# Turning of gathered rows in a mixture-of-experts kernel: the next tile's transposes ahead of a tile's last low parts, and one first output bank for every chunk

## The chip, the cores and the metric

The kernel runs on one core of one Trainium2 chip. The metric is the device time of one execution in microseconds (us), as the median over several executions; lower is better.

## The reference

The program is one attention layer with a sliding window, whose output feeds a mixture of experts with two experts per row. All arrays are float32.

```python
B, H, S, D = 8, 8, 576, 64                     # attention; window 64, causal
attn = softmax(where(mask, q @ k.T / sqrt(D), -1e9))
x = (attn @ v) as 4608 rows of 512
noisy = x @ w_gate + log1p(exp(x @ w_noise)) * noise     # 8 experts
top2 = two best experts of each row, with softmax weights top2_w
for e in range(8):
    for k in range(2):
        mask = top2[:, k] == e
        h = maximum(x[mask] @ w1[e], 0.0)                # 512 -> 1024
        out[mask] += top2_w[mask, k, None] * (h @ w2[e]) # 1024 -> 512
```

## The kernel before

**Attention and routing.** The first third of the program computes attention block by block, stores the rows `X` to DRAM and builds, per expert, the list of its rows. Neither part is touched by the change.

**Experts in chunks.** Each expert's rows are worked off in chunks: expert 0 in three (384, 384 and 448 rows), experts 1 to 7 in two each, 576 rows (chunk 0) and 640 rows (chunk 1). The loop at line 1116 runs over the chunks. Each chunk has two phases on TensorE: `up` (line 822, hidden layer, matmuls over half a chunk: 288 or 320 columns) and `down` (line 958, output layer, matmuls over 512 columns, one tile of 128 rows after the other; chunk 0's last tile has 64 rows). Every product is made of three matmuls on split operands: high times high, low times high, high times low. A "high part" is a copy of a float32 tile rounded to the fast matmul type, written by ScalarE; the "low part" is the difference, written by VectorE. The first layer of experts 1 to 7 uses a seven-product scheme for 2x2 blocks: `XH` and `XL` hold seven blocks (sums and differences of quarters of the rows, and the quarters themselves), and `PRODUCT` says which block meets which weight block.

**Gather and turn.** While `up` of a chunk runs, `gather` (line 670) fetches the next chunk's rows by an indirect DMA into `xg`, writes them to DRAM (`xs`) and reads them back in another layout (`xc`). While `down` of a chunk runs, `turn` (line 719) makes the next chunk's `XH` and `XL` from `xc`, tile by tile (five tiles; `q` is the tile, `m` its rows). Its two steps per tile are
- `f` (line 728): two 32x32-block transposes on VectorE, `xc` to `tq` (line 737);
- `g` (line 745): the first high part on ScalarE (749), a difference on VectorE (750), the first low part (751), two more differences (752, 753), then the second high part on ScalarE (755) and the second low part on VectorE (756). Blocks 0 to 2 come out of the first parts, blocks 3 to 6 out of the second.

`tq` has one buffer, taken anew for each tile; `up` takes the same buffer for its own sums.

**Order of the work.** The order on every engine is the order in which the program issues. `spread` (line 77) sets side work between the steps of a main loop: it lays the items of a list evenly over a stretch of the steps. `turn` returns a list of steps, and the loop at line 1116 lays it over `down`, from `free` to 0.86 of its steps, together with (in chunk 1) the last two quarters of the next expert's weight split: high parts at line 242, low parts at line 234, sums at line 264. Each engine works off its own instructions in that order.

**Banks.** PSUM has eight banks of 128x512: three `z` banks, `v`, `y`, two `d` banks and one for attention. `up` uses `v` and `y` for products of their own: the first product of a chunk (product 2) goes to `v`, the second (product 5) to `y`. The output tiles of `down` go round a ring of three: `d0`, `d1` and `y` (line 1108, `ring` at line 818). Their results are taken out by ScalarE (line 997; the 64-row tile by 999 on ScalarE and 1000, 1001 on VectorE) and added to DRAM by an indirect DMA of POOL (line 919). `turns["d"]` counts on from chunk to chunk, so that the first bank of a chunk differs.

```python
def ring(name):
    turns[name] += 1
    return BANKS[name][turns[name] % len(BANKS[name])]
```

Of the kernel before, what the change touches and what calls it, by code (L numbers as in the profile page):

```python
# [8 lines left out]
F32 = mybir.dt.float32  # L9
# [21 lines left out]
HALF = WIDE // 2  # L31
# [24 lines left out]
def chunks(e):  # L56
    return CHUNKS if e else FIRST


def tiles(e, c):  # L60
    n = chunks(e)[c]
    return [(q, min(128, n - q * 128)) for q in range(-(-n // 128))]
# [25 lines left out]
def tile_kernel(ctx, tc, qT, kT, vx, vT, wgx, noise, w1, w2, out):  # L88
# [611 lines left out]
    def turn_first(c):  # L700
        if not X0:
            X0.extend(exa.tile([128, 7, 2, HALF], F32R, name=x).rearrange("p a k n -> p (a k n)") for x in ("xh", "xl"))
        o = c % 2 * KD * FIRST[-1]
        xh, xl = (x[:, o:o + KD * FIRST[-1]].rearrange("p (k n) -> p k n", k=KD) for x in X0)
        XH[0, c], XL[0, c] = xh, xl
        cur = {}

        def f(q, m):
            y = cur[q] = turn_bank()[:, :KD * m].rearrange("p (k m) -> p k m", k=KD)
            for k in range(KD):  # L710
                nc.tensor.transpose(y[:, k], XG[0, c, q][:m, k * 128:k * 128 + 128], ident[:m, :m])

        def g(q, m):
            h, l = (x[:, :, q * 128:q * 128 + m] for x in (xh, xl))
            nc.scalar.activation(h, cur[q], AF.Copy)
            nc.vector.tensor_tensor(l, cur[q], h.bitcast(F32), op=OP.subtract)
        return [lambda q=q, m=m, x=x: x(q, m) for q, m in tiles(0, c) for x in (f, g)]

    def turn(e, c):
        if e == 0:  # L720
            return turn_first(c)
        todo = {}

        def begin():
            todo["h"] = XH[e, c] = exa.tile([128, 7, 2, HALF], F32R, name="xh")
            todo["l"] = XL[e, c] = exa.tile([128, 7, 2, HALF], F32R, name="xl")

        def f(q, m):
            if q == 0:
                begin()  # L730
            w = m // 2
            t = todo[q] = EXB["p"].tile([128, 4 * HALF], F32, name="tq", bufs=1)
            v = t[:, :16 * w].rearrange("p (s x) -> p s x", s=8)
            for h in range(2):
                d = v[:, 2 - 2 * h:4 - 2 * h].rearrange("p s (k x) -> p (s k) x", k=2).rearrange("p k (t c) -> p t k c", c=32)
                a = h * (CHUNKS[c] // 64) + 2 * q
                nc.vector.transpose(d, XC[e, c][:, a:a + w // 32].rearrange("p t (k c) -> p t k c", c=32))  # L737

        def parts(q, m, s0, s1):
            w = m // 2  # L740
            a = todo[q][:, s0 * 2 * w:s1 * 2 * w].rearrange("p (a x) -> p a x", x=w)
            return (a, *(x.rearrange("p a k x -> p (a k) x")[:, 2 * s0 - 2:2 * s1 - 2, q * 64:q * 64 + w]
                         for x in (todo["h"], todo["l"])))

        def g(q, m):
            w = m // 2
            v = todo[q][:, :16 * w].rearrange("p (s x) -> p s x", s=8)
            a, h, l = parts(q, m, 1, 4)
            nc.scalar.activation(h, a, AF.Copy)  # L749
            nc.vector.tensor_tensor(v[:, 4:6], v[:, 0:1].to_broadcast([128, 2, 2 * w]), v[:, 1:3], op=OP.subtract)  # L750
            nc.vector.tensor_tensor(l, a, h.bitcast(F32), op=OP.subtract)  # L751
            nc.vector.tensor_tensor(v[:, 6], v[:, 1], v[:, 5], op=OP.subtract)
            nc.vector.tensor_tensor(v[:, 7], v[:, 3], v[:, 6], op=OP.subtract)  # L753
            a2, h2, l2 = parts(q, m, 4, 8)
            nc.scalar.activation(h2, a2, AF.Copy)  # L755
            nc.vector.tensor_tensor(l2, a2, h2.bitcast(F32), op=OP.subtract)  # L756
        return [lambda q=q, m=m, x=x: x(q, m) for q, m in tiles(e, c) for x in (f, g)]

    pair = []

# [13 lines left out]
    EXB, BANKS = {}, {}  # L774
# [41 lines left out]
    late, turns = [], {"z": 0, "d": 0}  # L816
# [4 lines that stand above are left out]
# [106 lines left out]
    def down_first(c):  # L927
        e = 0
        hh, hl, ht = HH.pop((e, c))
        wt = GW[e, c]  # L930
        w2h, w2l = W2["h"], W2["l"]
        for q, m in tiles(e, c):
            y = exa.tile([128, XW], F32, name="xg", bufs=XB)[:, :DM]
            p = ring("d")
            if m == 128:
                sl = slice(q * 128, q * 128 + m)
                for f in range(KF):
                    nc.tensor.matmul(p, lhsT=hh[f][:, sl], rhs=w2h[:, f, :], start=(f == 0), stop=False)
                    nc.tensor.matmul(p, lhsT=hh[f][:, sl], rhs=w2l[:, f, :], start=False, stop=False)
                    nc.tensor.matmul(p, lhsT=hl[f][:, sl], rhs=w2h[:, f, :], start=False, stop=(f == KF - 1))  # L940
                    if f < KF - 1:
                        yield
                nc.scalar.activation(y, p, AF.Copy, scale=wt[:, q:q + 1])
            else:

                for f in range(KF):
                    t = ht[f].rearrange("p s t -> p (s t)")
                    nc.tensor.matmul(p, lhsT=t, rhs=w2h[:, f, :], start=(f == 0), stop=False)
                    nc.tensor.matmul(p, lhsT=t, rhs=w2l[:, f, :], start=False, stop=(f == KF - 1))
                    if f < KF - 1:  # L950
                        yield
                nc.scalar.activation(y[:m], p[m:2 * m], AF.Copy)
                nc.vector.tensor_tensor(y[:m], y[:m], p[:m], op=OP.add)
                nc.vector.tensor_scalar(y[:m], y[:m], wt[:m, q:q + 1], None, op0=OP.mult)
            add_rows(e, c, q, m, y)
            yield

    def down(e, c):
        if e == 0:
            yield from down_first(c)  # L960
            return
        wt = GW[e, c]
        hb = HH.pop((e, c))
        w2h, w2l = W2["h"], W2["l"]
        order = (0, 4, 1, 5, 2, 6, 3, 7)
        size = dict(tiles(e, c))
        steps = [(0, 0, 4), None, (0, 4, 6), (1, 0, 2), None, (1, 2, 6), (0, 6, 8), (1, 6, 8)]
        steps += [(q, 0, 8) for q in size if q > 1]
        P_ = {}
        for s in steps:  # L970
            if not s:
                yield from late.pop(0)
                continue
            q, i0, i1 = s
            m = size[q]
            if i0 == 0:
                P_[q] = ring("d")
            p = P_[q]
            for i in range(i0, i1):
                f = order[i]  # L980
                a, b = dict(start=(i == 0), stop=False), dict(start=False, stop=(i == KF - 1))
                if m == 128:
                    h, l = (hb[:, x, f, q * 128:q * 128 + 128] for x in range(2))
                    nc.tensor.matmul(p, lhsT=h, rhs=w2h[:, f, :], **a)  # L984
                    nc.tensor.matmul(p, lhsT=h, rhs=w2l[:, f, :], start=False, stop=False)  # L985
                    nc.tensor.matmul(p, lhsT=l, rhs=w2h[:, f, :], **b)  # L986
                else:
                    t = hb[:, 0, f, q * 128:q * 128 + 2 * m]
                    nc.tensor.matmul(p, lhsT=t, rhs=w2h[:, f, :], **a)
                    nc.tensor.matmul(p, lhsT=t, rhs=w2l[:, f, :], **b)  # L990
                if i < KF - 1:
                    yield
            if i1 < KF:
                continue
            y = exa.tile([128, XW], F32, name="xg", bufs=XB)[:, :DM]
            if m == 128:
                nc.scalar.activation(y, p, AF.Copy, scale=wt[:, q:q + 1])  # L997
            else:
                nc.scalar.activation(y[:m], p[m:2 * m], AF.Copy)
                nc.vector.tensor_tensor(y[:m], y[:m], p[:m], op=OP.add)  # L1000
                nc.vector.tensor_scalar(y[:m], y[:m], wt[:m, q:q + 1], None, op0=OP.mult)
            add_rows(e, c, q, m, y)
            yield
# [46 lines left out]
    for j in range(NT + 3):  # L1050
        if j == TURN:
            for q, f in enumerate(turn(0, 0)):
                aux.setdefault(j + q // 2, []).append(f)
# [53 lines left out]
    d, z, v, y = ([mps.tile([128, 512], F32, name=f"ps_{x}{q}") for q in range(k)] for x, k in zip("dzvy", (2, 3, 1, 1)))  # L1107
# [8 lines left out]
    for n, (e, c) in enumerate(work):  # L1116
        nxt = work[n + 1] if n + 1 < len(work) else None
        last = c == len(chunks(e)) - 1
# [171 lines left out]
```

## Time and profile before

| what | us |
|---|---|
| median of 3 runs | 1079.51 |
| the three runs | 1073.28, 1079.51, 1079.69 |
| profiled execution: span from its first to its last instruction | 1070.0 |
| TensorE busy in the span | 994.8 (93%) |
| VectorE busy | 715.2 (67%) |
| ScalarE busy | 521.8 (49%) |

The profile is of one execution. The list of runs does not name it apart: what is on record of its own time is its span, 3.3 us under the shortest run and 9.5 us under the median. Attention fills the span up to about 300 us; `up` of expert 1 starts at 332 us; the last matmul starts at 1058.6 us.

In the rows, PE is TensorE, DVE is VectorE, ACT is ScalarE, SP is the engine that issues plain DMAs. `L737` is line 737 of the kernel before. `ps_y<-xh,WH` is a matmul that writes bank `y` from `xh` and weights `WH`. A matmul's busy time overlaps the next one's: the distance between two starts is what a matmul costs in a stream.

### The profile page before, as it was taken

Reading aid. Unit: us, or ns where it says so; the run is one execution under the profiler, and the core shown is the slowest. Engines: PE = TensorE matmul, PEld = TensorE weight load, DVE = VectorE, ACT = ScalarE, POOL = GpSimd, SP = SyncE. Lnnn points to the kernel's source line nnn. Section 1 sums busy time; section 2 is a strip of 40 time slices with the busy share of each in tenths; the row PEclk is TensorE's granted clock in tenths of the full one; section 3 lists DMA queues with packets and bytes.
Section 4 is the critical chain, followed back from the end, with each engine's and each line's share of the span. In section 5 each row is a group of like instructions: output and inputs, shape, how many; then the busy total and the mean of one; then the engine's idle time right before and its main releaser. Section 6 shows DMA issues by size and latency. Waiting matters only on the chain.

```text
span 1070.0 us, 22034 instructions
## 1 busy us (share of the span) xinstructions
PE 994.8 (93%) x8433; PEld 882.8 (83%) x8433; DVE 715.2 (67%) x1804; ACT 521.8 (49%) x1305; POOL 338.5 (32%) x465
## 2 busy tenths in 40 slices
PE   8787878779999999999999999999999999999995
PEld 8676767668788898889898889898889897989894
DVE  5688888684276667666776677677666866686630
ACT  4885666432244444544463446354644554454430
POOL 5436636333223141413132213222322323132202
PEclk9998998989999999999999999999999999999998
DMA  9987887874357653665377626762765385537303
GB/s 340 364 259 230 252 257 239 273 230 113 49 131 193 168 115 65 188 169 119 61 204 162 149 25 206 162 145 30 230 136 140 43 244 124 125 69 209 45 2 51
DMA packets 107235, 168.94 MB, mean 158 GB/s; under 512 B 13360, under 2 KB 57648, under 8 KB 105328
## 3 DMA queue, kind: packets, MB, share of 16 engines
q1 hardware_dynamic: 89968, 126.96, 38.7%
q0 software_dynamic: 17152, 40.48, 20.8%
q8 instruction: 68, 1.11, 0.4%
q14 instruction: 47, 0.39, 0.1%
HBM read 110.08 MB, written 57.32 MB: 156 GB/s over the span
## 4 chain that ended last, share of the span: by engine, by line
PE 42%; DVE 30%; ACT 8%; DMA 8%; issue 8%; POOL 1%; SPq 1%; DVEq 0%; POOLq 0%; ACTq 0%
PE ps_z L841 4%; PE ps_z L843 4%; PE ps_z L842 4%; DVE tq L737 4%; DVE WL L234 3%; ACT xh L755 3%; DVE xl L756 3%; DMA xc<-xs 3%; DVE xl L751 2%; PE ps_d L985 2%; PE ps_d L984 2%; PE ps_d L986 2%; DVE ws L264 2%; DVE pt L358 2%; DMA xs<-xg 2%
## 5 line engine op out<-in xcount | busy, mean ns | idle before, releaser
L919 POOL DMA_INDIRECT out_dram<-xg,los x70 | 111.1, 1587 | 423.7 <-ACT xg L997 364.5
L853 ACT ACTIVATE hb<-tq 128x288 fp32r<-128x288 f32 (+1 forms) x168 | 77.1, 459 | 144.4 <-DVE tq L872 138.7
L841 PE MATMUL ps_z<-xh,WH 128*128 128x288 f32 (+1 forms) x448 | 137.4, 307 | 0.9
L842 PE MATMUL ps_z<-xl,WH 128*128 128x288 f32 (+1 forms) x448 | 135.6, 303 | 0.0
L843 PE MATMUL ps_z<-xh,WL 128*128 128x288 f32 (+1 forms) x448 | 135.6, 303 | 0.0
L872 DVE TENSOR_TENSOR tq<-ps_z,tq 128x288 f32<-128x288 f32 (+1 forms) x168 | 79.3, 472 | 81.8 <-PE ps_z L843 76.4
L985 PE MATMUL ps_d<-w2l,hb 128*128 128x512 f32 x328 | 127.9, 390 | 0.0
L984 PE MATMUL ps_d<-w2h,hb 128*128 128x512 f32 x328 | 127.8, 390 | 0.0
L986 PE MATMUL ps_d<-w2h,hb 128*128 128x512 f32 x328 | 127.7, 389 | 0.0
L857 DVE SCALAR_TENSOR_TENSOR hb<-tq,hb 128x320 fp32r<-128x320 f32 (+2 forms) x168 | 75.5, 449 | 37.6 <-ACT hb L853 34.2
L675 POOL DMA_INDIRECT xg<-xrows,lxs x70 | 71.1, 1016 | 83.7 <-DMA xs<-xg 39.0
L841 PEld LDWEIGHTS ps_z<-xh,WH 128*128 128x128 f32 x448 | 84.8, 189 | 5.2 <-DVE tq L872 3.8
L842 PEld LDWEIGHTS ps_z<-xl,WH 128*128 128x128 f32 x448 | 84.8, 189 | 1.1
L755 ACT ACTIVATE xh<-tq 128x512 fp32r<-128x512 f32 (+1 forms) x70 | 42.7, 611 | 87.9 <-DVE tq L753 87.9
L843 PEld LDWEIGHTS ps_z<-xh,WL 128*128 128x128 f32 x448 | 84.7, 189 | 0.0
L756 DVE TENSOR_TENSOR xl<-tq,xh 128x512 fp32r<-128x512 f32 (+1 forms) x70 | 46.6, 666 | 47.4 <-ACT xh L755 47.4
L395 ACT ACTIVATE x<-ps_o,r 128x80 f32<-128x80 f32 x288 | 67.0, 348 | 15.2 <-DVE r L387 15.0
L986 PEld LDWEIGHTS ps_d<-w2h,hb 128*128 128x128 f32 x328 | 61.6, 188 | 13.0
L984 PEld LDWEIGHTS ps_d<-w2h,hb 128*128 128x128 f32 x328 | 61.6, 188 | 12.1
L985 PEld LDWEIGHTS ps_d<-w2l,hb 128*128 128x128 f32 x328 | 61.6, 188 | 11.8
L234 DVE TENSOR_TENSOR WL<-ws,WH 128x512 fp32r<-128x512 f32 x112 | 66.5, 613 | 3.8 <-ACT WH L242 3.4
L749 ACT ACTIVATE xh<-tq 128x384 fp32r<-128x384 f32 (+1 forms) x70 | 35.6, 508 | 68.0 <-DVE tq L737 68.0
(248 smaller groups left out, 2562.5 us busy)
## 6 DMA issues: line engine op xcount, KB each, us to landing
ws<-in_w_dram SPq DMA_DIRECT2D x14, 2048.0 KB
xs<-xg SPq DMA_DIRECT2D x63, 256.0 KB
vw<-in_vx_dram SPq DMA_DIRECT2D x36, 272.0 KB
out_dram<-zero SPq DMA_DIRECT2D x38, 256.0 KB
qc<-in_qT_dram SPq DMA_DIRECT2D x36, 256.0 KB
KW<-in_kT_dram SPq DMA_DIRECT2D x36, 256.0 KB
vt<-in_vT_dram SPq DMA_DIRECT2D x36, 256.0 KB
xrows<-x SPq DMA_DIRECT2D x36, 256.0 KB
```

The source lines that it names most:

```text
L234: eng.tensor_tensor(l, x, h.bitcast(F32), op=OP.subtract)
L756: nc.vector.tensor_tensor(l2, a2, h2.bitcast(F32), op=OP.subtract)
L841: nc.tensor.matmul(p[:, :n], lhsT=WH[:, a, k, w], rhs=xh[:, b, k, :n], start=first and k == 0, stop=False, **free)
L842: nc.tensor.matmul(p[:, :n], lhsT=WH[:, a, k, w], rhs=xl[:, b, k, :n], start=False, stop=False, **free)
L843: nc.tensor.matmul(p[:, :n], lhsT=WL[:, a, k, w], rhs=xh[:, b, k, :n], start=False, stop=(k == 1), **free)
L853: nc.scalar.activation(hh[:, f, a:b], src, AF.Relu)
L857: nc.vector.scalar_tensor_tensor(hl[:, f, a:m], src[:, :m - a], 0.0, hh[:, f, a:m].bitcast(F32), op0=OP.max, op1=OP.subtract)
L872: nc.vector.tensor_tensor(t, a[:, :n], t, op=OP.add)
L919: s = nc.gpsimd.indirect_dma_start(out=out[:(2 + seen.get((e, c), NT)) * 128], out_offset=bass.IndirectOffsetOnAxis(ap=LT[e, c][1][q][:m], ...
L984: nc.tensor.matmul(p, lhsT=h, rhs=w2h[:, f, :], **a)
L985: nc.tensor.matmul(p, lhsT=h, rhs=w2l[:, f, :], start=False, stop=False)
L986: nc.tensor.matmul(p, lhsT=l, rhs=w2h[:, f, :], **b)
```

## The change

`turn` is written in another order, with three steps per tile in place of two, and the tile `tq` is taken once per chunk. The second high part and the second low part of a tile become a step of their own, `last`; the transposes `f` of the next tile are issued between `g` and `last` of a tile. The list has 15 items where it had 10, laid over the same stretch of `down`. In `down`, the count of the ring `d` is set to 2 at the start of every chunk, so that tiles 0 to 4 go to `d0`, `d1`, `y`, `d0`, `d1`.

```diff
@@ turn
         def f(q, m):
             if q == 0:
                 begin()
+                todo["t"] = EXB["p"].tile([128, 4 * HALF], F32, name="tq", bufs=1)
             w = m // 2
-            t = todo[q] = EXB["p"].tile([128, 4 * HALF], F32, name="tq", bufs=1)
+            t = todo["t"]
...
             nc.vector.tensor_tensor(v[:, 6], v[:, 1], v[:, 5], op=OP.subtract)
             nc.vector.tensor_tensor(v[:, 7], v[:, 3], v[:, 6], op=OP.subtract)
+
+        def last(q, m):
             a2, h2, l2 = parts(q, m, 4, 8)
             nc.scalar.activation(h2, a2, AF.Copy)
             nc.vector.tensor_tensor(l2, a2, h2.bitcast(F32), op=OP.subtract)
-        return [lambda q=q, m=m, x=x: x(q, m) for q, m in tiles(e, c) for x in (f, g)]
+        todo_list = tiles(e, c)
+        out_ = [lambda: f(*todo_list[0])]
+        for i, (q, m) in enumerate(todo_list):
+            out_.append(lambda q=q, m=m: g(q, m))
+            if i + 1 < len(todo_list):
+                out_.append(lambda i=i: f(*todo_list[i + 1]))
+            out_.append(lambda q=q, m=m: last(q, m))
+        return out_
@@ down
         P_ = {}
+        turns["d"] = 2
         for s in steps:
```

In the changed kernel the lines move: 737 becomes 738, 749 to 753 become 750 to 754, 755 and 756 become 758 and 759, 997 becomes 1008, 841 becomes 851, 986 becomes 996.

**VectorE, in `down` of a chunk 0, two tiles in the middle of the turn.** Before:

```order
L737 STREAM_TRANSPOSE tq<-xc 128x2x4x32 x2
L750 TENSOR_TENSOR tq<-tq 128x256
L751 TENSOR_TENSOR xl<-tq,xh 128x6x64
L752 TENSOR_TENSOR tq<-tq 128x128
L753 TENSOR_TENSOR tq<-tq 128x128
L756 TENSOR_TENSOR xl<-tq,xh 128x8x64
L737 STREAM_TRANSPOSE tq<-xc 128x2x4x32 x2
L750 TENSOR_TENSOR tq<-tq 128x256
```

Now:

```order
L738 STREAM_TRANSPOSE tq<-xc 128x2x4x32 x2
L759 TENSOR_TENSOR xl<-tq,xh 128x8x64
L751 TENSOR_TENSOR tq<-tq 128x256
L752 TENSOR_TENSOR xl<-tq,xh 128x6x64
L753 TENSOR_TENSOR tq<-tq 128x128
L754 TENSOR_TENSOR tq<-tq 128x128
L738 STREAM_TRANSPOSE tq<-xc 128x2x4x32 x2
L759 TENSOR_TENSOR xl<-tq,xh 128x8x64
```

The transposes of the next tile now stand between a tile's last difference (753, now 754) and its second low part (756, now 759).

**VectorE and ScalarE at the end of the turn, in `down` of a chunk 1, where the weight split (234, 242, 264) runs beside it.** VectorE's last tile (64 rows) before:

```order
L737 STREAM_TRANSPOSE tq<-xc 128x128 x2
L234 TENSOR_TENSOR WL<-ws,WH 128x4x128
L750 TENSOR_TENSOR tq<-tq 128x128
L751 TENSOR_TENSOR xl<-tq,xh 128x6x32
L752 TENSOR_TENSOR tq<-tq 128x64
L753 TENSOR_TENSOR tq<-tq 128x64
L756 TENSOR_TENSOR xl<-tq,xh 128x8x32
L234 TENSOR_TENSOR WL<-ws,WH 128x4x128 x3
```

Now:

```order
L738 STREAM_TRANSPOSE tq<-xc 128x128 x2
L264 TENSOR_TENSOR ws<-ws 128x2x128
L759 TENSOR_TENSOR xl<-tq,xh 128x8x64
L234 TENSOR_TENSOR WL<-ws,WH 128x4x128
L751 TENSOR_TENSOR tq<-tq 128x128
L752 TENSOR_TENSOR xl<-tq,xh 128x6x32
L753 TENSOR_TENSOR tq<-tq 128x64
L754 TENSOR_TENSOR tq<-tq 128x64
L234 TENSOR_TENSOR WL<-ws,WH 128x4x128
L759 TENSOR_TENSOR xl<-tq,xh 128x8x32
L234 TENSOR_TENSOR WL<-ws,WH 128x4x128 x2
```

One low part of the weights (234) now stands ahead of the very last low part of the turn. ScalarE over the last two tiles before:

```order
L749 ACTIVATE xh<-tq 128x6x64
L755 ACTIVATE xh<-tq 128x8x64
L242 ACTIVATE WH<-ws 128x4x128 x2
L997 ACTIVATE xg<-ps_d_3967,wg 128x512
L749 ACTIVATE xh<-tq 128x6x32
L755 ACTIVATE xh<-tq 128x8x32
L242 ACTIVATE WH<-ws 128x4x128 x2
L997 ACTIVATE xg<-ps_y_3972,wg 128x512
L867 ACTIVATE tq<-ps_v_3971 128x288
```

Now:

```order
L750 ACTIVATE xh<-tq 128x6x64
L758 ACTIVATE xh<-tq 128x8x64
L242 ACTIVATE WH<-ws 128x4x128 x2
L750 ACTIVATE xh<-tq 128x6x32
L1008 ACTIVATE xg<-ps_d_3966,wg 128x512
L242 ACTIVATE WH<-ws 128x4x128
L758 ACTIVATE xh<-tq 128x8x32
L242 ACTIVATE WH<-ws 128x4x128
L1008 ACTIVATE xg<-ps_d_3967,wg 128x512
L877 ACTIVATE tq<-ps_v_3971 128x288
```

An output tile's copy (997, now 1008) stands between the first and the second high part of the last tile. The last output tile is taken from `d1` (3967), where this chunk took it from `y` (3972).

## Rows read from the trace of the kernel before

**Rows 1.** The page's head: the span, and TensorE's busy time.
```profile
span 1070.0 us, 22034 instructions
PE 994.8 (93%) x8433; PEld 882.8 (83%) x8433; DVE 715.2 (67%) x1804; ACT 521.8 (49%) x1305; POOL 338.5 (32%) x465
```

**Rows 2.** TensorE's waits, 400 to 1070 us: released by, total us, times, longest.
```profile
PE ps_y L841 <- DVE xg L1000: 3.2, 2, 1.6
PE ps_y L841 <- ACT xg L997: 3.1, 2, 1.5
PE ps_v L842 <- DVE xl L751: 1.8, 8, 0.3
PE ps_y L842 <- DVE xl L756: 0.6, 2, 0.3
```

**Rows 3.** Stretches of 7 us after a `down`'s end: TensorE busy (matmuls), clock, DMA.
```profile
330.08:337.08 7.00, 4.93 (x25) 0.76 0.49 70
381.92:388.92 7.00, 7.00 (x48) 1.00 0.43 63
434.61:441.61 7.00, 5.21 (x23) 0.76 0.57 129
...
539.22:546.22 7.00, 6.65 (x43) 1.00 0.61 132
588.59:595.59 7.00, 5.24 (x22) 0.76 0.41 56
...
694.47:701.47 7.00, 6.68 (x44) 1.00 0.47 63
747.75:754.75 7.00, 5.23 (x34) 1.00 0.56 131
...
900.69:907.69 7.00, 5.29 (x33) 1.00 0.46 56
...
1005.06:1012.06 7.00, 6.30 (x37) 1.00 0.39 47
```

**Rows 4.** All engines in order of time, 434 to 439 us.
```profile
434.40 0.39 PE L986 MATMUL ps_y<-w2h,hb 128*128 128x512 f32 x1
434.76 0.40 PE L841 MATMUL ps_v<-xh,WH 128*128 128x288 f32 x1
...
435.41 0.40 PE L842 MATMUL ps_v<-xl,WH 128*128 128x288 f32 x1 [0.25 <-DVE xl L751]
...
436.23 0.42 DVE L756 TENSOR_TENSOR xl<-tq,xh 128x256 fp32r<-128x256 f32 x1 [0.49 <-ACT xh L755]
436.57 1.89 DVE L234 TENSOR_TENSOR WL<-ws,WH 128x512 fp32r<-128x512 f32 x3
437.14 0.67 ACT L997 ACTIVATE xg<-ps_y,wg 128x512 f32<-128x512 f32 x1
...
437.86 0.43 PE L841 MATMUL ps_y<-xh,WH 128*128 128x288 f32 x1 [1.54 <-ACT xg L997]
...
438.10 0.43 PE L842 MATMUL ps_y<-xl,WH 128*128 128x288 f32 x1
```

**Rows 5.** VectorE in order of time, 579 to 584 us: one tile of the turn.
```profile
579.53 0.77 DVE L737 STREAM_TRANSPOSE tq<-xc 128x256 f32<-128x256 f32 x2
580.34 0.42 DVE L750 TENSOR_TENSOR tq<-tq 128x256 f32<-128x256 f32 x1
580.89 0.56 DVE L751 TENSOR_TENSOR xl<-tq,xh 128x384 fp32r<-128x384 f32 x1
...
582.68 0.69 DVE L756 TENSOR_TENSOR xl<-tq,xh 128x512 fp32r<-128x512 f32 x1 [0.70 <-ACT xh L755]
583.40 0.77 DVE L737 STREAM_TRANSPOSE tq<-xc 128x256 f32<-128x256 f32 x2
```

**Rows 6.** VectorE's waits, 400 to 1070 us, columns as in rows 2.
```profile
DVE xl L756 <- ACT xh L755: 40.6, 60, 0.7
DVE tq L737 <- DMA xc<-xs: 7.4, 5, 2.2
```

More of the change, by code (lines that the diff above doesn't have):

```diff
@@ L740, in parts @@
             w = m // 2
-            a = todo[q][:, s0 * 2 * w:s1 * 2 * w].rearrange("p (a x) -> p a x", x=w)
+            a = todo["t"][:, s0 * 2 * w:s1 * 2 * w].rearrange("p (a x) -> p a x", x=w)
             return (a, *(x.rearrange("p a k x -> p (a k) x")[:, 2 * s0 - 2:2 * s1 - 2, q * 64:q * 64 + w]
@@ L746, in g @@
             w = m // 2
-            v = todo[q][:, :16 * w].rearrange("p (s x) -> p s x", s=8)
+            v = todo["t"][:, :16 * w].rearrange("p (s x) -> p s x", s=8)
             a, h, l = parts(q, m, 1, 4)
```

## The prediction

> **What bounds the kernel now.** I read the head of the page first: TensorE is busy for 994.8 us of a span of 1070.0 [rows 1], so only what keeps TensorE waiting can be won. TensorE's waits from 400 us on, where experts run without attention beside them, come next: they name two things, bank `y`, whose old output tile has not been taken out (3.2 + 3.1 us in four places), and the low parts of the turn, lines 751 and 756 (1.8 + 0.6 us) [rows 2]. All stand at the start of an `up`. That column is small, 8.7 us in all, but it counts idle time between a modelled end and the next start, and a matmul of 0.40 us costs only about 0.13 us in a stream: in the timeline L842 follows L841 after 0.65 us, and the wait column gives 0.25 of it [rows 4]. The loss is 0.52.
>
> So I counted matmuls. The third view cuts 7 us from the end of each `down` (14 places, one per chunk of experts 1 to 7) and gives the matmuls in each [rows 3]. Undisturbed, at 320 columns, it is 48 (0.146 us each; three stretches are like the one at 381.92). At 288 columns that makes 48 x 320/288 = 53 (0.132 us each). What is missing is the loss:
> - 288 columns: 330.08: 28 missing, 3.7 us; 434.61: 30, 4.0; 747.75: 19, 2.5; 539.22: 10, 1.3, and three more like it (41 to 43 matmuls), 5.7 for the four. Sum 15.9.
> - 320 columns: 588.59: 26, 3.8; 694.47: 4, 0.6; 900.69: 15, 2.2; 1005.06: 11, 1.6; the three full ones 0. Sum 8.2.
>
> Together 24.1 us. In three stretches the granted clock is 0.76, which is 3.4 us at the lower level (1.2 GHz) and the rest at 2.4; TensorE had stood still just before, for 1.54 us at 437.86, and the matmuls behind the wait come 0.24 us apart, where 0.13 is usual [rows 3, 4]. Two waits as long (747.75, 900.69) had no such dip. Where it comes it adds about 1.7 us, and it is in the 24.1.
>
> The Trainium skill (Perfetto Trace Analysis, Tensor Engine Instruction) says that a matmul's end in a profile is estimated from its size, not observed. This case agrees: starts 0.13 us apart with durations of 0.29 and more. By the idle column alone the change could bring at most 8.7 us.
>
> **The change part by part.** *The bank.* Tiles of a chunk now end in `d1`, and `y` serves tile 2 only, whose copy has two tiles of matmuls to be done in. The next `up` asks for `d1` nowhere, and the next `down` uses it as its second bank. So the four waits for `y` go, at no cost: no instruction is added. What is then late is the low part for product 5, as in the stretches of the same kind that had no bank wait: 1.3 at 288 columns, 0.6 at 320. Net: (4.0 - 1.3) + (2.5 - 1.3) + (3.8 - 0.6) + (2.2 - 0.6) = 8.7 us, clock dips included.
>
> *The transposes ahead.* A tile of the turn takes 583.40 - 579.53 = 3.87 us on VectorE, of which 0.70 is standing still for the second high part [rows 5]; 60 such waits make 40.6 us [rows 6]. The next tile's two transposes take 580.34 - 579.53 = 0.81 us and need nothing from ScalarE, so they fill that hole. A turn of five tiles has four such places: its last tile comes 4 x 0.70 = 2.8 us earlier. (L751 also waits 0.1 to 0.2 us for the first high part; ScalarE can now write it while VectorE does the low part before. I count nothing for it.) Beside the weight split in a chunk 1, VectorE has the same holes and no others of note, so the 2.8 us hold there too.
>
> What was late? L751 of the last tile let L842 start at 435.41, due at 434.76: 0.65 us. The last L756 ends at 436.65; product 5 needs it six matmuls after 434.63, at 435.4: 1.2 us late [rows 4]. In the new order one L234 (1.89/3 = 0.63 us) stands ahead of it, so it comes 2.8 - 0.6 = 2.2 us earlier, 1.0 us in time. At 1005.06 the whole loss is 1.6, at 330.08 it is 3.7 with the clock dip, about 2.0 of waiting: all below 2.8. So the rest of the 24.1, 15.4 us, goes too.
>
> *What could hold it back.* ScalarE's copy of an output tile now stands ahead of some second high parts, and waits there for that tile's last matmul. For the first two tiles of a turn this costs VectorE about as much as the hole did before; from the third on the output tile has long been done. I cost it at zero, with 1.3 us a place as the upper bound (a rival below). One tile `tq` for the chunk adds no wait: the transposes write its first half, the pending low part reads the second. SP's and POOL's orders are unchanged.
>
> Not all of it will go to zero; I leave 0.1 us at each of 14 places. Sum: 24.1 - 1.4 = 22.7 us, from a span of 1070.0 to 1047.3. The runs lie 3.3 (shortest) to 9.7 us above that span, the median 9.5; against the median the forecast is 1079.5 - 22.7 = **1057 us**. What can be told from no change in this kernel is about 1%, 10.8 us.
>
> **The rivals.**
> *Only the bank counts.* If the last tile of the turn is not brought forward, because ScalarE's order and not VectorE's hole sets its pace, 8.7 us are left: 1070.8 us, within 1%. For it: ScalarE stands behind its own copies (L997 starts at 437.14, 2.5 us after its tile's matmuls [rows 4]). Against it: ScalarE is busy half the span only [rows 1], and each hole ends as soon as L755 does [rows 5].
> *Transfers come late.* In five turns VectorE waited for `xc` to land, up to 2.2 us [rows 6]. With TensorE faster, the gather has less time. If every 320-column `up` then loses as much as the one at 1005.06 now, that is 7 x 1.6 = 11.2 in place of 0.7, and the gain is 12.2: 1067.3 us. Against it: the gather starts behind the copy of the last output tile, which also comes earlier (it need not wait until 437.14).
> *The turn's end comes later: slower.* If the copy (0.67) and the low part (0.63) now ahead of the last second parts [rows 4] only push them back, and nothing is won before, product 5 waits 1.3 us longer at 14 places, 18.2 us, less the bank's 8.7: 1079.5 + 9.5 = 1089 us. It decides where the turn comes forward by less than 1.3 us; the holes of 0.70 four times over speak against it. The Trainium skill (Perfetto Trace Analysis, same section) calls ScalarE and VectorE strictly first in, first out, which is what this rival lives on; the late L997 agrees [rows 4].
>
> **How the numbers follow.** Forecast 0.77, only the bank 0.11, transfers 0.08, slower 0.04. Faster by over 1%: 0.77 + 0.08 = 0.85; within 1%: 0.11; slower: 0.04. The range goes down by the 6.2 us that lie between the shortest run and the median, and by some 5 us for the hole that L751 waits in and for clock dips that a median run may have more of than the profiled one (1057 - 11 = 1046), and up to the case of late transfers, 1068; above it lie some 0.15.
>
> **What would show it.** Right: no wait of TensorE for `y` behind L1008 or L1011 of the changed kernel; 47 to 53 matmuls in each of the 14 stretches, clock 1.00 in all; VectorE's wait for the second high part gone from most of its 60 places, a tile of the turn in about 3.1 us; the span near 1047. Wrong: L852 still waiting for L752 at a chunk's start (the turn was not brought forward), VectorE's first transposes waiting longer than 2.2 us for `xc` (transfers), or product 5 waiting for L759 (the low part pushed back).

## The result, and the profile after

| | median, us | runs | ratio to before (95% interval) |
|---|---|---|---|
| before | 1077.54 | 1073.28 to 1079.69 (4) | |
| changed kernel | **1052.9** | 1048.88 to 1055.64 (4) | 0.9759 (0.9723 to 0.9795) |

The change wins 24.6 us by the medians. The profiled execution took 1048.88 us, with a span of 1047.1: 22.9 less than in [rows 1].

The page's head, span and busy times:

```profile
span 1047.1 us, 22033 instructions
PE 985.3 (94%) x8433; PEld 881.9 (84%) x8433; DVE 708.9 (68%) x1804; ACT 522.2 (50%) x1305; POOL 336.9 (32%) x465
```

The same matmuls, and the same work on the other engines. TensorE's busy time fell by 9.5 us, though no matmul was taken out. The Trainium skill (Perfetto Trace Analysis, Identifying the Most-Contended Engine) calls matmul busy time a poor measure of how near a kernel is to its limit; this case agrees, since the busy share moved by one point (93% to 94%) where the span moved by 2.1%.

Stretches of 7 us after a `down`'s end, as in [rows 3] (stretch, length, TensorE busy with the count of matmuls, clock, DMA share, GB/s); the other stretches read alike:

```profile
332.41:339.41 7.00, 7.00 (x54) 1.00 0.56 81
380.41:387.41 7.00, 7.00 (x49) 1.00 0.46 63
432.98:439.98 7.00, 7.00 (x54) 1.00 0.95 276
581.41:588.41 7.00, 7.00 (x49) 1.00 0.45 62
734.49:741.49 7.00, 7.00 (x54) 1.00 0.94 263
883.24:890.24 7.00, 7.00 (x49) 1.00 0.42 62
```

Where [rows 3] had 22 to 48 matmuls there are 49 at 320 columns and 54 at 288, which is the full count (the window takes one more at its edge), and the clock is 1.00 in all. TensorE's waits from 332 us to the end have one row left, where [rows 2] had four:

```profile
PE ps_v L851 <- ACT tq L877: 0.3, 1, 0.3
```

VectorE's waits, 380 to 1047 us (total, times, longest):

```profile
DVE tq L738 <- DMA xc<-xs: 9.7, 6, 2.2
DVE xl L759 <- ACT xh L758: 7.2, 12, 0.8
```

The wait for the second high part was 40.6 us in 60 places [rows 6] and is 7.2 us in 12. The wait for `xc` rose only from 7.4 to 9.7 us and its longest stayed at 2.2: transfers did not become the bound. Two tiles of the turn on VectorE, in order of time:

```profile
573.85 0.69 DVE L759 TENSOR_TENSOR xl<-tq,xh 128x512 fp32r<-128x512 f32 x1 [0.80 <-ACT xh L758]
574.57 0.43 DVE L751 TENSOR_TENSOR tq<-tq 128x256 f32<-128x256 f32 x1
574.92 0.55 DVE L752 TENSOR_TENSOR xl<-tq,xh 128x384 fp32r<-128x384 f32 x1
...
576.03 0.77 DVE L738 STREAM_TRANSPOSE tq<-xc 128x256 f32<-128x256 f32 x2
576.73 0.67 DVE L759 TENSOR_TENSOR xl<-tq,xh 128x512 fp32r<-128x512 f32 x1
577.43 0.43 DVE L751 TENSOR_TENSOR tq<-tq 128x256 f32<-128x256 f32 x1
```

The transposes at 576.03 stand where VectorE stood still [rows 5]. From one L751 to the next it is 577.43 - 574.57 = 2.86 us, against 3.87 for a tile before. Not every tile gains so much: the one ahead of it, which ends with the hole of 0.80 at 573.85, took 3.75. Two more holes are left in this turn, 0.46 in the first tile and 0.70 in the last, which has no next tile to fill it. The end of a turn, all engines, at the place that [rows 4] show of before:

```profile
430.14 0.35 DVE L752 TENSOR_TENSOR xl<-tq,xh 128x192 fp32r<-128x192 f32 x1
...
431.41 0.42 DVE L759 TENSOR_TENSOR xl<-tq,xh 128x256 fp32r<-128x256 f32 x1
...
433.00 0.29 PE L851 MATMUL ps_v<-xh,WH 128*128 128x288 f32 x1
...
433.25 0.69 ACT L1008 ACTIVATE xg<-ps_d,wg 128x512 f32<-128x512 f32 x1 [1.38 <-issue]
...
433.79 0.29 PE L851 MATMUL ps_y<-xh,WH 128*128 128x288 f32 x1
```

The last low part is done at 431.83, 1.2 us before `up` starts; before it was done 2.0 us after (436.65 and 434.63). The copy of the last output tile starts at 433.25, 0.25 us into the phase, where it came 2.5 us into it at 437.14. Product 5 starts at 433.79 with no wait; that copy reads bank `d1`, so nothing here asks for it. Whether it would have been in time for bank `y` as well is what the first experiment asks.

**Two measures.** The window counts are coarse (one matmul is 0.13 us or more), so the experiments use two finer ones. *Loss at the starts*: from each `down`'s end over 8 us, the distances between matmul starts, less 0.2275, 0.1467 or 0.1325 us (the undisturbed distances at 512, 320 and 288 columns), added up over the 14 starts. *Experts' part*: from where the first `up` of expert 1 is due (0.23 us after the start of the `down` matmul ahead of it; in the kernel before it started 2.2 us later than that) to the start of the last matmul. It leaves out what comes ahead, attention and expert 0, whose length differs between executions by up to 10 us (the start column below). Both are read from one profiled execution of each kernel. Against the changed kernel the two agree within 0.5 us in all rows but experiments 3 and 6 (finer steps, weights wider), where what differs lies inside the phases.

| kernel | starts of 288 columns | of 320 | loss, us | experts' part, us | against the changed kernel |
|---|---|---|---|---|---|
| before | 17.0 | 9.2 | 26.2 | 330.10 to 1058.55: 728.45 | +25.4 |
| changed | 0.35 | 0.25 | 0.6 | 332.43 to 1035.48: 703.05 | |
| order alone | 0.9 | 2.0 | 3.0 | 334.88 to 1040.29: 705.41 | +2.4 |
| bank alone | 13.35 | 10.35 | 23.7 | 340.46 to 1066.37: 725.91 | +22.9 |
| finer steps, old order | 2.3 | 8.0 | 10.4 | 333.79 to 1051.92: 718.13 | +15.1 |
| low part twice | 11.7 | 5.7 | 17.4 | 335.14 to 1054.47: 719.33 | +16.3 |
| new order every second turn | 15.7 | 2.0 | 17.7 | 329.99 to 1050.01: 720.02 | +17.0 |
| weights laid wider | 0.35 | 0.25 | 0.6 | 333.16 to 1031.96: 698.80 | -4.25 |

From before to the changed kernel the loss fell by 25.6 us and the experts' part by 25.4: all that was won was won at the 14 starts.

### The profile page after: what moved, and what is told of

It reads as the page before. It is cut to its first block, busy times and chain, and to the rows that moved or that the text cites. A ratio compares the mean times of both kernels' runs of the same rounds, so it can differ in the third digit from the quotient of the medians.

```text
span 1047.1 us, 22033 instructions
## 1 busy us (share of the span) xinstructions
PE 985.3 (94%) x8433; PEld 881.9 (84%) x8433; DVE 708.9 (68%) x1804; ACT 522.2 (50%) x1305; POOL 336.9 (32%) x465
## 3 DMA queue, kind: packets, MB, share of 16 engines
q8 instruction: 68, 1.11, 0.5%
## 4 chain that ended last, share of the span: by engine, by line
PE 79%; DVE 10%; ACT 4%; issue 3%; POOL 2%; DMA 1%; SPq 0%; POOLq 0%; ACTq 0%; DVEq 0%
PE ps_d L996 8%; PE ps_d L995 8%; PE ps_d L997 8%; PE ps_z L851 6%; PE ps_z L853 5%; PE ps_z L852 5%; PE ps_o L376 3%; PE ps_v L851 3%; PE ps_y L996 2%; PE ps_y L997 2%; PE ps_y L995 2%; PE ps_v L853 2%; PE ps_v L852 2%; PE ps_y L851 2%; PE ps_y L853 2%
## 5 line engine op out<-in xcount | busy, mean ns | idle before, releaser
L996 PE MATMUL ps_d<-w2l,hb 128*128 128x512 f32 x392 | 152.9, 390 | 0.0
L995 PE MATMUL ps_d<-w2h,hb 128*128 128x512 f32 x392 | 152.8, 390 | 0.0
L997 PE MATMUL ps_d<-w2h,hb 128*128 128x512 f32 x392 | 152.6, 389 | 0.0
L882 DVE TENSOR_TENSOR tq<-ps_z,tq 128x288 f32<-128x288 f32 (+1 forms) x168 | 79.3, 472 | 87.7 <-PE ps_z L853 83.6
L997 PEld LDWEIGHTS ps_d<-w2h,hb 128*128 128x128 f32 x392 | 73.6, 188 | 15.5
L995 PEld LDWEIGHTS ps_d<-w2h,hb 128*128 128x128 f32 x392 | 73.6, 188 | 14.1
L996 PEld LDWEIGHTS ps_d<-w2l,hb 128*128 128x128 f32 x392 | 73.6, 188 | 13.8
L341 POOL TENSOR_TENSOR t<-t,mx 128x512 f32<-128x512 f32 x36 | 38.0, 1056 | 92.2 <-DVE mx L340 72.2
L376 PE MATMUL ps_o<-vw,pt 64*64 64x85 f32 x2176 | 56.0, 250 | 12.0 <-issue 7.6
```

The lines of the kernel that those rows point to most:

```text
L376: nc.tensor.matmul(PO[j][u * 64:u * 64 + 64, a, g * 2 + x, :], lhsT=pt[pa, w, u * 2 + g, x * 64:x * 64 + 64], rhs=v[pa, (i + w) % 2, :, u, ...
L882: nc.vector.tensor_tensor(t, a[:, :n], t, op=OP.add)
```

## The experiments

Each kernel was timed in several runs beside runs of the kernel before on the same chip; ratios are to before (medians 1076.8 us for the first four, 1079.19 for the last two).

**1. The order alone.** The changed kernel without the fixed first bank:

```diff
         P_ = {}
-        turns["d"] = 2
```

> The changed kernel without the fixed first bank: tiles end in y again in four of the fourteen places. Theory A, the prediction's own sum: the wait for bank y is a cost of its own, so the four places lose 1.2 to 3.2 us each as before and 8.7 us come back; span about 1047.1 + 8.7 = 1056, TensorE waiting for y some 1.5 us four times. Theory B: the copy of the last output tile was only late because it stood behind the turn's last parts and the weight split on ScalarE and VectorE. In the changed kernel ScalarE is free when that tile's matmuls end (433.25 us, 0.25 after the next phase starts), so the copy is done 0.2 us after product 5 is due at 288 columns and about 0.8 us after at 320 columns: 2 x 0.3 + 2 x 0.9 = 2.4 us; span about 1049.5, four waits for y of under 1 us.

Measured: median 1051.64 us (1049.36 to 1054.56), ratio 0.9752 (0.9718 to 0.9786), the same as the changed kernel within what can be told. In the experts' part it is 2.4 us behind it. Stretches after a `down`'s end, in two of the four chunks that begin after a last tile in `y`:

```profile
435.42:442.42 7.00, 6.96 (x51) 1.00 0.97 271
584.12:591.12 7.00, 6.37 (x43) 1.00 0.39 57
```

and TensorE's waits with the place at 584 us:

```profile
PE ps_y L851 <- DVE xg L1010: 1.3, 2, 0.6
PE ps_v L851 <- ACT tq L877: 0.3, 1, 0.3
```

```profile
584.39 0.59 ACT L1009 ACTIVATE xg<-ps_y 64x512 f32<-64x512 f32 x1 [2.17 <-PE ps_y L1000]
...
585.07 0.68 DVE L1010 TENSOR_TENSOR xg<-xg,ps_y 64x512 f32<-64x512 f32 x1 [2.13 <-ACT xg L1009]
...
585.81 0.41 PE L851 MATMUL ps_y<-xh,WH 128*128 128x320 f32 x1 [0.63 <-DVE xg L1010]
```

Bank `y` is still asked for too early, but by 0.9 us at 320 columns (twice) and 0.36 us at 288 (twice), where before the losses there were 2.3 to 4.1 us. The copies behind the waits of 1.5 us and more in [rows 2] were late because they stood on ScalarE and VectorE behind the late turn; with the turn done early they start sooner. So the bank's wait was for the most part an effect of the turn, and the order removes it.

**2. The bank alone.** The kernel before with the line `turns["d"] = 2` in `down`, and nothing else.

> The kernel before with the fixed first bank alone. Theory A and the hole theory: the four waits for y go, the waits for the low parts of the turn stay: about 8.7 us less than before, 15.4 us more than the changed kernel; span about 1061 to 1062; in the fourteen stretches of 7 us, 41 to 44 matmuls at 288 columns (fewer at 330 us, where there is no bank wait), 36 to 48 at 320. Theory B says the same for this kernel's banks. Rival (banks are all): the fourteen stretches are full, 47 to 53 matmuls, and the span is near 1047.

Measured: median 1074.88 us (1067.04 to 1079.58, 12 runs), ratio 0.9963 (0.9933 to 0.9993): a gain of 4 us (0.75 to 7) by the ratio, 1.9 by the medians and 2.5 in the experts' part, where 8.7 were expected. Stretches after a `down`'s end:

```profile
445.03:452.03 7.00, 6.65 (x43) 1.00 0.60 119
494.40:501.40 7.00, 6.50 (x40) 1.00 0.45 56
597.63:604.63 7.00, 6.31 (x38) 1.00 0.41 50
804.59:811.59 7.00, 6.03 (x35) 1.00 0.38 44
```

At the four bank places the loss fell as forecast in kind: 4.07 to 1.53 us, 2.61 to 1.53, 3.96 to 1.63 and 2.29 to 1.97, together 6.3 us. By the last section's figures for the lower clock, 1.5 + 1.7 = 3.2 of these are an effect of it: it came at two of the four places before and at none here. But three starts of 320 columns that lost little or nothing before now lose 1.31, 1.52 and 2.07 (0.14, 0.74 and 0.13 before): 3.9 us go back. The reason is in VectorE's first transposes of the turn between 445 and 494 us, and its waits from 380 us on:

```profile
477.23 0.77 DVE L737 STREAM_TRANSPOSE tq<-xc 128x256 f32<-128x256 f32 x2 [1.66 <-DMA xc<-xs]
```

```profile
DVE xl L756 <- ACT xh L755: 43.4, 64, 0.7
DVE tq L737 <- DMA xc<-xs: 12.3, 6, 2.4
```

The turn starts 477.23 - 445.03 = 32.2 us after the `up` before it, held by the transfer; in the kernel before it started 33.0 us after. TensorE reaches the next `up` 17.2 us after that first transpose (494.40 - 477.23), where it took 18.9. A phase without its bank wait is shorter, the turn begins about when it did, and so it ends later against TensorE. All six turns that waited for `xc` here show it: the loss at the next start is that wait less 0.3 to 0.4 us (1.66 and 1.31 here, 2.35 and 2.07 at 804.59); the one turn into 640 rows that did not wait lost 0.14. The second high part is waited for in 64 places as before.

**3. Three steps, old order.** The changed kernel, with `last` of a tile listed before the next tile's transposes:

```diff
             out_.append(lambda q=q, m=m: g(q, m))
+            out_.append(lambda q=q, m=m: last(q, m))
             if i + 1 < len(todo_list):
                 out_.append(lambda i=i: f(*todo_list[i + 1]))
-            out_.append(lambda q=q, m=m: last(q, m))
```

> The changed kernel with the transposes of the next tile behind the second low part again, but with the list of fifteen steps, the one tile for the chunk and the fixed first bank. Hole theory: in the turns without a weight split beside them (into the 320-column phases) VectorE still stands still for 0.7 us per tile and these starts lose what they lose with the banks alone, 0.6 us each and more at the last; in the turns beside the weight split one or two sums (0.34 us each) now fall into the hole, so the last tile comes some 1.6 us earlier there and about 0.2 us a place is left. Together about 5 us more than the changed kernel, span about 1052. Rival (the finer steps are all): as the changed kernel, 1047. Rival (the transposes are all, the finer steps nothing): as the banks alone, 1061 to 1062.

Measured: median 1065.11 us (1059.48 to 1070.91), ratio 0.9882 (0.984 to 0.9925); 15.1 us behind the changed kernel in the experts' part, where 5 were expected. Stretches, two of 288 and two of 320 columns, and TensorE's waits:

```profile
436.30:443.30 7.00, 7.00 (x54) 1.00 0.74 226
743.56:750.56 7.00, 7.00 (x54) 1.00 0.79 185
793.00:800.00 7.00, 6.25 (x37) 1.00 0.30 39
896.36:903.36 7.00, 5.65 (x32) 1.00 0.29 39
```

```profile
PE ps_z L851 <- DVE tq L882: 2.8, 7, 0.9
PE ps_v L851 <- ACT tq L877: 2.0, 4, 0.5
```

At 288 columns all starts but the first are full: beside those turns runs the weight split, and with a tile in three steps some of its parts fall into VectorE's holes without any reordering. In the turn that ends at 436 us VectorE's waits for the second high part are 1.4 us in three places, where before they were 3.3 in five; the last low part is done 0.4 us after `up` starts, 1.6 earlier than before (2.0), and product 5 asks for it 0.8 us after. At 320 columns no weight split runs beside the turn, every tile keeps its hole of 0.70, and 8.0 us are lost. How much a start loses there goes by the transfer, as in experiment 2; the turn ahead of the worst one, at 896.38, begins with

```profile
880.73 0.77 DVE L738 STREAM_TRANSPOSE tq<-xc 128x256 f32<-128x256 f32 x2 [3.21 <-DMA xc<-xs]
```

and the loss is that wait less 0.8 us (3.21 and 2.43; 1.28 and 0.51, 1.89 and 1.11, and so in all six that waited), and 0.04 where the turn did not wait. The changed kernel waits for `xc` too, up to 2.2 us, and loses nothing: where a turn begins 2.2 us late there, it takes 15.5 us from the first transposes to the last low part; a late one takes 18.9 here and 19.3 in the kernel before. So at 320 columns the transposes ahead make room for late transfers; no run moved the transfers themselves, and this rests on the losses of the twelve starts in experiments 2 and 3 that follow such a wait.

The starts make 9.8 of the 15.1 (10.4 - 0.6); the other 5 lie in waits inside the phases (TensorE's two rows above), whose cause was not tried by itself. So part of what the prediction gave to the order of transposes is, in every second turn, an effect of the finer steps (with the one `tq` for the chunk, which was not tried by itself); in the other half the transposes ahead are needed.

**4. The second low part twice.** The changed kernel, with the subtraction of `last` issued two times in a row; the result is the same, VectorE has 0.7 us more per tile (0.42 for the 64-row tile).

```diff
             nc.vector.tensor_tensor(l2, a2, h2.bitcast(F32), op=OP.subtract)
+            nc.vector.tensor_tensor(l2, a2, h2.bitcast(F32), op=OP.subtract)
```

> The changed kernel with every second low part of the turn written twice: about 0.65 us more on VectorE per tile. It measures how much the turn may slip before TensorE waits. From the changed kernel's rows: the last tile's first low part is done 2.6 us before it is needed at 288 columns and 3.3 us at 320, the last second low part 2.0 and 2.1 us. Hole theory: four extra low parts push the first by 2.6 us (just in time), five push the second by about 3.2 us: product 5 waits about 1.2 us in fourteen places, 14 to 18 us in all, span 1061 to 1065. Rival (VectorE is not what sets the turn's pace): no change, 1047. Rival (each wait also costs a dip of the clock): up to 14 x (1.2 + 1.7) = 40 us, 1087.

Measured: median 1067.67 us (1063.04 to 1075.03), ratio 0.99 (0.9865 to 0.9934); 16.8 us more loss at the starts, 16.3 in the experts' part. TensorE's waits, 329 to 1060 us:

```profile
PE ps_y L853 <- DVE xl L760: 7.3, 14, 1.0
PE ps_v L853 <- DVE xl L752: 1.6, 6, 0.7
```

Product 5 waits for the doubled low part at all 14 starts. VectorE sets the turn's pace, and the room that the change left is about 2 us: the last low part is done 1.2 us before `up` and needed 0.8 us after it; 4 x 0.67 + 0.42 = 3.1 us more overran that by 1.1, and 14 times 1.1 is 15. Measured by start it was 1.5 us at 288 columns (2.8 at the first) and 0.5 to 1.45 at 320.

**5. The new order in every second turn.** The kernel of experiment 1, but with the old order and two steps in the turns into the 576-row chunks:

```diff
         out_ = [lambda: f(*todo_list[0])]
+        if c == 0:
+            return [lambda q=q, m=m, x=x: x(q, m) for q, m in todo_list for x in (f, lambda q, m: (g(q, m), last(q, m)))]
         for i, (q, m) in enumerate(todo_list):
```

> The transposes of the next tile ahead only in turns whose rows go into a chunk of 640 (the turns with no weight split beside them); the other turns and the banks as before. Theory B with the hole theory: the seven starts at 320 columns are full but for two with 0.9 us for bank y; the seven at 288 columns lose what they lost before, 16 to 17 us; together about 18 us more than the changed kernel, span about 1065. Rival (what is won at one start is lost at the next, as with the banks alone): the starts at 320 columns lose 1 us or more each, and the span is 1070 or more.

Measured: median 1069.09 us (1063.56 to 1074.39), ratio 0.9915 (0.9886 to 0.9944); 17.0 us behind the changed kernel in the experts' part. Stretches, two of 288 and two of 320 columns:

```profile
433.19:440.19 7.00, 5.22 (x34) 1.00 0.61 129
741.02:748.02 7.00, 5.22 (x24) 0.77 0.62 140
...
585.63:592.63 7.00, 6.37 (x43) 1.00 0.46 64
792.97:799.97 7.00, 7.00 (x49) 1.00 0.45 63
```

Each half of the starts answers to its own turns: 15.7 us are lost at 288 columns (17.0 before, with the lower clock at two starts where here it came at one), and 2.0 at 320, nearly all of it bank `y`'s 0.92 in two places, as in experiment 1. The gain at one kind of start is not given back at the other, unlike in experiment 2, because here the turn itself is shorter.

**6. The weight split laid wider.** Most of what the changed kernel still loses lies inside `up` of a chunk 1 (experts 1 to 6; expert 7 has no next weights to split): there VectorE's weight sums (L264) stand ahead of the sum that empties a `z` bank (L882), and TensorE waits. Its rows at the first such place, in the changed kernel:

```profile
395.73 0.43 DVE L264 TENSOR_TENSOR ws<-ws 128x256 f32<-128x256 f32 x1
396.08 0.48 DVE L882 TENSOR_TENSOR tq<-ps_z,tq 128x320 f32<-128x320 f32 x1
...
396.16 0.31 PE L853 MATMUL ps_z<-xh,WL 128*128 128x320 f32 x1
...
396.61 0.42 PE L851 MATMUL ps_z<-xh,WH 128*128 128x320 f32 x1
```

The starts are 0.45 us apart where 0.15 is usual. The edit lays the first quarter of the next expert's weight split over more steps of that phase:

```diff
-            parts += ([(0.55, 0.75, nextw[0]), (0.8, 1.0, nextw[1])] if e else
+            parts += ([(0.5, 0.78, nextw[0]), (0.8, 1.0, nextw[1])] if e else
```

> The changed kernel with the first part of the next expert's weight split laid over 0.5 to 0.78 of a chunk's first phase in place of 0.55 to 0.75. In the changed kernel TensorE loses 0.3 us once in each 320-column phase, 16 us after its start, because VectorE works off weight parts before the sum that frees bank z. Thinned out, the parts leave the sum in time: some 0.3 us less at six places, about 1.8 us, span about 1045. Rival (the wait only moves to another sum): no change, 1047.

Measured: median **1045.63 us** (1044.13 to 1047.69, 6 runs), ratio 0.9705 (0.9674 to 0.9736). All six runs are below the shortest of the changed kernel (1048.88); the intervals of the two ratios still overlap a little (0.9723 to 0.9736). The experts' part is 4.25 us shorter, where 1.8 were expected. That place now:

```profile
396.80 0.31 PE L853 MATMUL ps_z<-xh,WL 128*128 128x320 f32 x1
396.95 0.31 PE L851 MATMUL ps_z<-xh,WH 128*128 128x320 f32 x1
```

Here the matmuls start 0.15 us apart, and TensorE has no wait listed from 332 us to the end. The gain is more than twice 1.8 because each late start of 0.31 us was followed by three more, of 0.11 to 0.12 us: 0.65 per chunk, 3.9 over the six. The rest is the one wait that the changed kernel's row for `ps_v` lists (0.34 us, at 853.78), which is gone too; why was not tried. This kernel is shorter than the changed one and the one before.

## Why the prediction was right, and where its working failed

**The total.** 22.7 us were forecast; the span fell by 22.9, the experts' part by 25.4, the medians by 24.6. The median of 1052.9 lies 4.1 under the forecast of 1057 and inside its range. Of these 4.1, 2.0 are the base (the median before is 1077.54 with a fourth run, not 1079.51), and the rest is that the losses were a little larger than the count of matmuls gave: 26.2 by the distances of starts against 24.1. With nearly nothing left of them (0.6, where 1.4 was allowed) the gain came out higher. The total did not rest on how the loss was split: it was the sum of what 14 starts lost, and all of it went.

**The failed step: the split into 8.7 for the bank and 15.4 for the order.** The net of 8.7 was worked out by taking the bank's wait away and leaving what stood behind it. Alone the bank brought 2.5 us, and on top of the order 2.4; the order alone brought 728.45 - 705.41 = 23.0. Two things were wrong in it. The wait for `y` was counted as the bank's own, though the copy that frees it stood on ScalarE and VectorE behind the turn (experiment 1). And the four places were treated as independent of the other ten, while a shorter phase gives the next turn less time (experiment 2). The rival of late transfers had that mechanism, but for the whole change, where it did not happen. The 15.4 had a third thing wrong in it: what 320 columns lost outside the bank's two places (0.74 at 694.47, 1.80 at 1005.06) was put down to VectorE's holes, where it goes by the transfer: the turns ahead of them had waited 1.09 and 2.16 us for `xc`, and the three that waited 0.31 or less lost 0.13 or 0.14.

**The holes of 0.70 us.** Four per turn gave at least their 2.8 us. The last low part came 2.0 + 1.2 = 3.2 us earlier against the start of `up` at the place of [rows 4], where 2.2 was worked out. A tile into 640 rows now takes 2.85 to 3.76 us instead of 3.87, up to 1.0 less where 0.70 was worked out; the long ones are those that wait for ScalarE's copy, below. That three steps alone already fill more than half of the holes in turns into 288 columns, which is enough there (experiment 3), was not seen: the prediction read the holes beside the weight split as needing the transposes.

**ScalarE's copies ahead of second high parts, costed at zero.** Right for the time, but not for the reason given, that from the third on the output tile has long been done. ScalarE in a turn of the changed kernel:

```profile
572.61 0.69 ACT L1008 ACTIVATE xg<-ps_y,wg 128x512 f32<-128x512 f32 x1 [1.85 <-PE ps_y L997]
573.20 0.62 ACT L758 ACTIVATE xh<-tq 128x512 fp32r<-128x512 f32 x1
...
578.05 0.69 ACT L1008 ACTIVATE xg<-ps_d,wg 128x512 f32<-128x512 f32 x1 [0.68 <-PE ps_d L997]
```

It waits for TensorE to finish the tile, and the second high part starts only behind that copy; the hole of 0.80 at 573.85 on VectorE comes from it. The turn is now in part paced by the output tiles: into 640 rows it takes 17.75 us where it begins on time (361.49) and 15.5 where it begins 2.2 us late. That costs nothing, because the last low part is done 1.2 us before `up` all the same. The strict order of ScalarE and VectorE, which the Trainium skill states (Perfetto Trace Analysis, Tensor Engine Instruction) and on which the slower rival rested, is seen here too: the copy at 572.61 holds the high part behind it, whose input was done at 572.24.

**The rivals.** Only the bank: refuted, the order is nearly all. Late transfers: 9.7 us of waits for `xc`, longest 2.2, and all starts of 320 columns full; refuted for the changed kernel, whose shorter turn takes up the lateness, though in experiments 2 and 3 the losses at 320 columns go by it. Slower: the copy and the weight part do stand ahead of the last parts, but the turn came forward by 3.2 us, more than the 1.3 from which it would have decided; experiment 4 shows that 3.1 us more on VectorE would have cost 16 of the 25.

## What to carry to other kernels

Where a chain goes back and forth between two in-order engines, put the next tile's independent step into the hole of this tile's chain; look first whether finer steps let other work fall into it. A wait for a buffer is not the buffer's cost until it is known why the one that frees it came late: here most of it was a queue behind late work. And to size a loss at a phase's start, add up the distances between matmul starts; waits listed for TensorE from 400 us on gave 8.7 us where 22 were lost (26.2 less 4.1 at the two starts ahead of that).

## What was not expected of the hardware

- The lower clock follows some waits and not others of the same length. Over the profiled executions, five of nine waits of 1.5 to 2.1 us at a phase's start were followed by a granted clock of 0.76 or 0.77 over 7 us (at 330, 434 and 588 us before, at 342 in experiment 2, at 744 in experiment 5), four were not (747 and 900 before, 332 and 436 in experiment 5); none followed a wait of 1.04 us or less. Where it came it cost about 1.5 us at 288 columns (4.07 at 434.61 against 2.61 at 747.75, both before) and 1.7 at 320 (3.96 at 588.59 against 2.29 at 900.69), and the losses in the table hold it. Why some and not others stays open; no kernel tried it.
- The part ahead of expert 1, attention and expert 0, ended between 330.0 and 340.5 us in the eight profiled executions. The runs of one kernel spread by 4 to 12 us, so this part alone could make most of that; the experts' part leaves it out and tells a change of 2 us that the medians can't.
